# Gated recurrence and tanh-shrink layer: score matmuls of a level issued head by head in turn

## The chip, the cores and the metric

The kernel runs on one core of one Trainium2 chip. The metric is the device time of one execution in microseconds, the median of several runs. A core has five engines that work at the same time, each on its own queue of instructions in order: TensorE (PE in the profile; its weight loads are shown apart as PEld), VectorE (DVE), ScalarE (ACT), GpSimd (POOL) and SyncE (SP, which here only starts DMAs).

## The reference

There are two blocks. The first is a gated linear recurrence over 768 tokens for 4 batches of 8 heads with 48 features each. The second is a dense layer from 384 to 2048 and back, with h - tanh(h) between.

```python
for t in range(S):
    state = alpha[:, :, t, :, None] * state + einsum('bhd,bhe->bhde', k[:, :, t], v[:, :, t])
    y[:, :, t] = einsum('bhd,bhde->bhe', q[:, :, t], state)
x = y.transpose(0, 2, 1, 3).reshape(B * S, H * D)      # (3072, 384)
h = x @ w_in                                           # w_in (384, 2048)
out = (h - tanh(h)) @ w_out                            # w_out (2048, 384)
```

All arithmetic is fp32. The weights come as float64 and are rounded to fp32 on the chip.

## The kernel before

**Tiling.** The 3072 tokens are cut into 12 units of 256 tokens (two chunks of 128). For each unit, `gla(u)` computes the recurrence and leaves x with features on the partitions (`xT`), and `moe(u)` runs the dense layer on it. `load(u)` starts the DMAs of a unit, and `weights()` loads and converts the two weight matrices once, while the first units run.

**The recurrence.** A head's 48 features are padded to 64 rows, so that two heads lie on the 128 partitions: even heads (`hh` = 0) on rows 0 to 63, odd heads (`hh` = 1) on rows 64 to 127. Two chunks by four pairs of heads give G = 8 groups. `flip` transposes alpha, k and q into `pre`, `kT` and `qT`. Within a chunk, the decays between tokens are built by halving, in seven levels. At each level:

- VectorE forms `W` from `qT` times `pre` (L209) and `kT` times `suf` (L213);
- TensorE multiplies, for each of 8 groups and each half of the rows, 64 by 128 weights from `W` with 64 columns of `W` (L220), into a PSUM tile `sc` that holds 8 groups of 64 columns, one whole bank;
- VectorE copies the entries that the mask selects from `sc` into `scores` (L225), once for even and once for odd heads;
- GpSimd brings `suf` and `pre` to the next level (L234, L235).

The pool `ps_sc` has two buffers, so a level's tile for even heads takes the buffer that the level before used for its even heads, and so for odd heads. All eight PSUM banks are in use. After the levels, `scores` and the state from chunk to chunk are multiplied with q and v into `y` (L246, L249), and the state is carried on (L261 to L279).

**The dense part.** `moe(u)` has eight steps. Each makes `h` for 256 of the 2048 hidden features (L292: 12 TensorE instructions), computes h - tanh(h) by a polynomial on ScalarE and VectorE (L301 to L310), and, two steps later, adds to the output tiles `o` (L317: 8 instructions).

**Order.** A list written out at the end of the kernel interleaves the pieces: the recurrence of unit u is handed over beside the dense steps of unit u - 1. The framework's scheduler then fixes each engine's order of instructions at build time and inserts the semaphores; it may move an independent instruction ahead of another. At run time each engine follows that order.

Of the kernel before, what the change touches and what calls it, by code (L numbers as in the profile page):

```python
# [8 lines left out]
FP32 = mybir.dt.float32  # L9
I32 = mybir.dt.int32  # L10
# [4 lines left out]
PSUM = bass.MemoryType.PSUM  # L15

P = 128
HP = 64         # rows that a head's features take up on the partitions
CU = 2          # chunks of 128 tokens in a unit

# h - tanh(h) = h u Q(u) with u = h h. Q to the last bit of fp32 for u <= U_MAX; past that
# the difference itself has lost little.
U_MAX = 0.25
C0, C1, C2, C3, C4 = 0.3333333280927353, -0.1333322737626519, 0.05393378726557631, -0.021472710399165713, 0.006946984308285347
ZA = C4 ** 0.5
# [5 lines left out]
def kernel(  # L31
# [11 lines left out]
    B, H, S, D = q.shape  # L43
    HD = H * D
    NP = H // 2
    G = CU * NP
    TU = CU * P
    UPB = S // TU
# [15 lines left out]
    ps_sc = ctx.enter_context(tc.tile_pool(name="ps_sc", bufs=2, space=PSUM))  # L64
# [5 lines left out]
    V, A, T, GP = nc.vector, nc.scalar, nc.tensor, nc.gpsimd  # L70
# [5 lines left out]
    m_bias = consts.tile([P, 1], FP32, name="m_bias")  # L76
    V.memset(m_bias, -U_MAX)

    # mask[s, l, t]: token s is in the left half of the block of 2 << l whose right half has
    # t, the t-th token of right halves.  # L80
    mask = consts.tile([P, LEVELS, P // 2], FP32, name="mask")
    GP.memset(mask, 1.0)
    for l in range(LEVELS):
        L = 1 << l
        m = mask[:, l, :].rearrange("p (n j) -> p n j", j=L)
        n = P // (2 * L)
# [2 lines left out]
        GP.affine_select(out=m, in_=m, compare_op=ALU.is_ge, fill=0.0, base=L - 1,  # L89
                         pattern=[[2 * L, n], [0, L]], channel_multiplier=-1)  # L90

    # What only parts of are written later: features past D of a head, scores of s >= t, and
    # the state between the heads of a pair stay 0.
    nat = [[consts.tile([P, CU, H, HP], FP32, name=f"{n}{i}") for n in ("an", "kn", "qn")]
           for i in range(2)]
    for i in range(2):
# [2 lines left out]
    scores = [consts.tile([P, 2, G, P], FP32, name=f"scores{i}") for i in range(2)]  # L99
# [7 lines left out]
    w_out = consts.tile([P, FT, d_model], FP32, name="w_out")  # L107

    def load_w(dst, src):
        """A part of a weight matrix, of up to 512 columns: from float64 rounded to fp32, with  # L110
        what fp32 has no normal number for as 0 or infinite."""
        if moe_w_in.dtype == FP32:
            nc.sync.dma_start(out=dst, in_=src)
            return
        n = dst.shape[-1]
        raw = two.tile([P, 512], I64, name="raw")
        nc.sync.dma_start(out=raw[:, 0:n], in_=src)
        words = raw.bitcast(I32).rearrange("p (n w) -> p n w", w=2)
        lo, hi = words[:, 0:n, 0].bitcast(mybir.dt.uint32), words[:, 0:n, 1]
        e = two.tile([P, 512], I32, name="e", tag="u")[:, 0:n]  # L120
        m = two.tile([P, 512], I32, name="m", tag="z")[:, 0:n]
        low = two.tile([P, 512], FP32, name="low", tag="t")[:, 0:n]
        man = two.tile([P, 512], FP32, name="man", tag="w")[:, 0:n]
        V.tensor_scalar(out=e, in0=hi, scalar1=20, scalar2=0x7FF,  # L124
                        op0=ALU.logical_shift_right, op1=ALU.bitwise_and)
        V.tensor_scalar(out=e, in0=e, scalar1=896, scalar2=1151, op0=ALU.max, op1=ALU.min)
        V.tensor_scalar(out=e, in0=e, scalar1=23, scalar2=0x3FFFFFFF,  # L127
                        op0=ALU.logical_shift_left, op1=ALU.bitwise_and)
        V.scalar_tensor_tensor(out=e, in0=hi, scalar=-0x40000000, in1=e,  # L129
                               op0=ALU.bitwise_and, op1=ALU.bitwise_or)  # L130
        V.tensor_single_scalar(out=m, in_=hi, scalar=0xFFFFF, op=ALU.bitwise_and)  # L131
        A.activation(man, m, AF.Copy, bias=1.0, scale=2.0 ** -20)
        A.activation(low, lo, AF.Copy, scale=2.0 ** -52)
        GP.tensor_add(man, man, low)
        V.tensor_mul(dst, man, e.bitcast(FP32))

    def weights():
        """In the order in which the first unit needs them."""
        w = 512
        for i in range(d_ff // w):  # L140
            for j in range(KT):
                load_w(w_in[:, j, i * w:(i + 1) * w], w_in_r[:, j, i * w:(i + 1) * w])
            yield
            for f in range(i * w // P, (i + 1) * w // P):
                load_w(w_out[:, f, :], w_out_r[:, f, :])
            yield
# [3 lines left out]
    def load(u):  # L150
        b, i = divmod(u, UPB)
        vt = three.tile([P, CU, H, D], FP32, name="vt")
        for c in range(CU):
            t0 = i * TU + c * P
# [8 lines left out]
    xT = {}  # L163

    def gla(u):
        """x of a unit's tokens, features on the partitions. Within a chunk of 128 tokens, s and
        t > s part at one level of halving: s in a block's left half, t in its right one. The
        decay between them is then one product from the middle to t times one from s to the
        middle, each of factors that the recurrence itself multiplies."""
        b, i = divmod(u, UPB)  # L170
        an, kn, qn = nat[u % 2]
        vt = loaded.pop(u)
# [2 lines left out]
        def unit(name, pool=two):  # L175
            return pool.tile([P, CU, NP, P], FP32, name=name)

        def halves(t, L):
            x = t.rearrange("p c g (n two j) -> p (c g n) two j", two=2, j=L)
            return x[:, :, 0, :], x[:, :, 1, :]  # L180

        def flip(dst, src, copy):
            tp = ps_tp.tile([P, NP, P], FP32, name="tp")
            for g in range(NP):
                T.transpose(tp[:, g, :], src[:, 2 * g:2 * g + 2, :], ident)  # L185
            copy(dst, tp)

        pre, suf, qT, kT = unit("pre"), unit("suf"), unit("qT"), unit("kT")
        for c in range(CU):
            flip(pre[:, c], an[:, c], V.tensor_copy)  # L190
            flip(kT[:, c], kn[:, c], A.copy)
            flip(qT[:, c], qn[:, c], A.copy)
        # s = t
        qk = two.tile([P, CU * H, D], FP32, name="qk")
        dv = two.tile([P, CU * H, D], FP32, name="dv")
        dot = two.tile([P, CU * H], FP32, name="dot")
# [7 lines left out]
        for l in range(LEVELS):  # L204
            L = 1 << l
            W = unit("W")
            (W0, W1), (k0, _), (_, q1) = halves(W, L), halves(kT, L), halves(qT, L)
            (p0, p1), (s0, s1) = halves(pre, L), halves(suf, L)
            V.tensor_mul(W1, q1, p1)  # L209
            if l == 0:  # L210
                A.copy(W0, k0)
            else:
                V.tensor_mul(W0, k0, s0)  # L213
            Wh = W.rearrange("p c g (n two j) -> p (c g) n two j", two=2, j=L)
            Wf = W.rearrange("p c g t -> p (c g) t")
            for hh in range(2):
                rows = slice(HP * hh, HP * hh + HP)
                sc = ps_sc.tile([P, G, P // 2], FP32, name="sc")
                for g in range(G):
                    T.matmul(sc[:, g, :], lhsT=Wf[rows, g, :], rhs=Wh[rows, g, :, 1, :],  # L220
                             start=True, stop=True)
                to = P_[:, hh].rearrange("p g (n two j) -> p g n two j", two=2, j=L)[:, :, :, 1, :]
                n = P // (2 * L)
                on = mask[:, l, :].rearrange("p (n j) -> p n j", j=L).bitcast(I32)
                V.copy_predicated(  # L225
                    out=to, mask=on.unsqueeze(1).to_broadcast([P, G, n, L]),
                    data=sc.rearrange("p g (n j) -> p g n j", j=L))
            e0 = p0[:, :, L - 1:L].to_broadcast(list(p0.shape))
            e1 = p1[:, :, L - 1:L].to_broadcast(list(p1.shape))
            if l == 0:  # L230
                GP.tensor_copy(s0, p1)
                GP.memset(s1, 1.0)
            else:
                GP.tensor_mul(s0, s0, e1)  # L234
            GP.tensor_mul(p1, p1, e0)  # L235
            yield

        x_t = xT[u] = two.tile([P, KT, TU], FP32, name="xT")
        for c in range(CU):
            n = i * CU + c  # L240
            old, new = states[n % 2], states[(n + 1) % 2]
            y = ps_y.tile([P, HD], FP32, name="y", tag="y")
            if n > 0:
                V.tensor_mul(qT[:, c], qT[:, c], pre[:, c])
                for g in range(NP):
                    T.matmul(y[:, 2 * g * D:2 * (g + 1) * D], lhsT=qT[:, c, g, :],  # L246
                             rhs=old[:, g, :], start=(g == 0), stop=False, skip_group_check=True)
            for h in range(H):
                T.matmul(y[:, h * D:(h + 1) * D], lhsT=P_[:, h % 2, c * NP + h // 2, :],  # L249
                         rhs=vt[:, c, h, :], start=(n == 0 and h == 0), stop=True,  # L250
                         skip_group_check=True)
            x = two.tile([P, HD], FP32, name="x")
# [14 lines left out]
            up = ps_y.tile([P, NP, 2 * D], FP32, name="up", tag="y")  # L267
            for g in range(NP):
                T.matmul(up[:, g, :], lhsT=ks[:, g, :],  # L269
                         rhs=vt[:, c, 2 * g:2 * g + 2, :], start=(g == 0), stop=(g == NP - 1),  # L270
                         skip_group_check=True)
            for hh in range(2):
                at = (slice(HP * hh, HP * hh + HP), slice(None), slice(D * hh, D * hh + D))
                if n == 0:
                    V.tensor_copy(new[at], up[at])
                    continue
                end = pre[at[0], c, :, P - 1:P].to_broadcast([HP, NP, D])
                GP.tensor_mul(new[at], old[at], end)  # L278
# [51 lines left out]
            nc.sync.dma_start(out=out_r[u * CU + c], in_=ob)  # L330
        yield

    # The order in which instructions are handed to the scheduler: a unit's own recurrence runs
    # while the unit before it is in the dense part.
    MOE, GLA, EARLY = FS + 1, 1 + LEVELS + 2 * CU, 5.0
    order = []
    for u in range(NU):
        order += [(u * MOE + i, 1, "moe", u) for i in range(MOE)]
        at = (u - 1) * MOE - EARLY
# [39 lines left out]
```

## Time and profile before

| | |
|---|---|
| Median of 3 runs | 1139.68 us (1138.49 to 1145.95) |
| Profiled execution, span | 1140.3 us; no other time of this execution is given |
| Instructions | 14741 |
| TensorE matmul busy | 1045.0 us (92%) |
| VectorE busy | 805.0 us (71%) |
| GpSimd busy | 342.8 us (30%) |
| ScalarE busy | 320.6 us (28%) |
| Mean granted TensorE clock | 0.909 of full |
| Score matmuls (L220) | 2688 instructions, 305 ns mean each, 338.1 us busy |
| Copies out of the score tiles (L225) | 168 of 882 ns mean, 147.8 us busy |

Busy time is the union of the times in which an engine had an instruction in progress. Matmuls overlap in the pipeline, so the mean time of one is longer than the pitch from one to the next. "Granted clock" is the share of TensorE's full clock that the chip allowed. In lists of waits, the engine and line on the left waited for those on the right: microseconds in total, how often, the longest. A row of the timeline gives the start, the length, the engine, the line, the operation and the count of instructions merged into it.

### The profile page before, as it was taken

What the parts mean: (1) busy time and instruction counts of PE and PEld (TensorE: products, weight loads), DVE (VectorE), ACT (ScalarE), POOL (GpSimd) and SP (SyncE); (2) the same over time, 40 slices, a digit from 0 to 9 for tenths busy, and PEclk for the clock granted to TensorE, in tenths of its full rate; (3) what the DMA queues carried; (4) which work ended last, traced back from release to release, by engine and by line L of the source; (5) the groups of instructions that cost most, each with busy time, mean ns of one, the idle gap of its engine ahead of it and who ended that gap; (6) DMA issues with size and microseconds to landing.
All of it is one profiled execution on the core that took longest, in us unless ns stands there. A gap on an engine that the chain in (4) does not pass through costs nothing.

```text
span 1140.3 us, 14741 instructions
## 1 busy us (share of the span) xinstructions
PE 1045.0 (92%) x5752; PEld 845.6 (74%) x5752; DVE 805.0 (71%) x1212; ACT 320.6 (28%) x569; POOL 342.8 (30%) x293
## 2 busy tenths in 40 slices
PE   3765648999999999999999999999999999999988
PEld 2764548877877878778777788778787788777765
DVE  6688896584684677776774777685775676776766
ACT  2012330321421331421511431521502322413433
POOL 6454443043042044043132043143132152141000
PEclk9999755887998899989988999998979999989999
DMA  9433620110110020110200110200200000000000
GB/s 175 81 91 97 150 73 1 27 30 14 27 31 14 1 56 15 29 28 15 56 1 15 35 23 14 50 8 14 56 1 15 1 1 15 1 1 15 1 14 14
DMA packets 107396, 37.11 MB, mean 33 GB/s; under 512 B 100672, under 2 KB 103744, under 8 KB 107328
## 3 DMA queue, kind: packets, MB, share of 16 engines
q1 hardware_dynamic: 107328, 36.19, 14.1%
q8 instruction: 45, 0.74, 0.3%
q14 instruction: 23, 0.19, 0.1%
HBM read 31.46 MB, written 4.72 MB: 32 GB/s over the span
## 4 chain that ended last, share of the span: by engine, by line
PE 79%; DVE 15%; POOL 2%; issue 2%; ACT 1%; DMA 0%; SPq 0%; POOLq 0%; DVEq 0%
PE sc L220 24%; PE h L292 24%; PE o L317 20%; PE y L249 4%; DVE scores L225 3%; PE tp L185 2%; PE y L246 2%; PE up L269 2%; DVE e L129 1%; DVE W L209 1%; DVE z L307 1%; DVE e L127 1%; PE tp L265 1%; DVE m L131 1%; DVE e L124 1%
## 5 line engine op out<-in xcount | busy, mean ns | idle before, releaser
L220 PEld LDWEIGHTS sc<-W 64*128 64x128 f32 x2688 | 324.9, 217 | 92.7 <-issue 68.7
L220 PE MATMUL sc<-W 64*128 64x64 f32 x2688 | 338.1, 305 | 53.6 <-DVE W L213 41.0
L292 PE MATMUL h<-xT,w_in 128*128 128x256 f32 x1152 | 325.1, 426 | 5.1 <-DVE g L310 3.8
L317 PE MATMUL o<-w_out,g 128*128 128x384 f32 x768 | 278.7, 504 | 0.2 <-DVE g L310 0.2
L292 PEld LDWEIGHTS h<-xT,w_in 128*128 128x128 f32 x1152 | 231.7, 213 | 46.0 <-issue 4.8
L225 DVE COPY_PREDICATED scores<-mask,sc 128x512 f32<-128x512 int32 x168 | 147.8, 882 | 117.4 <-PE sc L220 115.1
L317 PEld LDWEIGHTS o<-w_out,g 128*128 128x128 f32 x768 | 147.5, 198 | 84.0 <-issue 7.7
L301 ACT ACTIVATE sq<-h 128x512 f32<-128x512 f32 x96 | 57.4, 598 | 440.9 <-PE h L292 437.1
L235 POOL TENSOR_TENSOR pre<-pre 128x512 f32<-128x512 f32 x84 | 118.3, 1409 | 115.5 <-DVE W L209 112.3
L234 POOL TENSOR_TENSOR suf<-suf,pre 128x512 f32<-128x512 f32 x72 | 100.3, 1393 | 140.3 <-DVE W L213 137.5
L305 DVE TENSOR_TENSOR w<-h,sq 128x512 f32<-128x512 f32 x96 | 66.2, 690 | 93.1 <-ACT th L302 92.4
L209 DVE TENSOR_TENSOR W<-qT,pre 128x512 f32<-128x512 f32 x84 | 60.1, 716 | 24.9 <-POOL pre L235 14.9
L310 DVE COPY_PREDICATED g<-large,h 128x512 f32<-128x512 int32 x96 | 70.6, 736 | 3.3
L309 DVE SCALAR_TENSOR_TENSOR g<-z,w 128x512 f32<-128x512 f32 x96 | 70.8, 737 | 1.8
L307 DVE SCALAR_TENSOR_TENSOR z<-z,sq 128x512 f32<-128x512 f32 x96 | 70.2, 731 | 0.0
L303 ACT ACTIVATE z<-sq,z_bias 128x512 f32<-128x512 f32 x96 | 69.6, 725 | 0.0
L304 ACT ACTIVATE large<-sq,m_bias 128x512 f32<-128x512 f32 x96 | 69.3, 722 | 0.0
L308 DVE SCALAR_TENSOR_TENSOR z<-z,sq 128x512 f32<-128x512 f32 x96 | 67.7, 705 | 1.9
L306 DVE TENSOR_TENSOR h<-h,th 128x512 f32<-128x512 f32 x96 | 66.7, 695 | 0.0
L213 DVE TENSOR_TENSOR W<-kT,suf 128x512 f32<-128x512 f32 x72 | 56.4, 784 | 14.2 <-POOL suf L234 14.2
L278 POOL TENSOR_TENSOR state<-state,pre 64x192 f32<-64x192 f32 x32 | 23.1, 722 | 139.3 <-DVE state L279 69.8
L249 PE MATMUL y<-vt,scores 128*128 128x48 f32 x384 | 53.2, 291 | 4.7 <-DVE scores L225 4.7
(60 smaller groups left out, 737.1 us busy)
## 6 DMA issues: line engine op xcount, KB each, us to landing
raw<-in_moe_w_in_dram SPq DMA_DIRECT2D x12, 512.0 KB, 3.9
raw<-in_moe_w_out_dram SPq DMA_DIRECT2D x16, 384.0 KB, 3.1
an<-in_alpha_dram SPq DMA_DIRECT2D x24, 192.0 KB, 3.3
kn<-in_k_dram SPq DMA_DIRECT2D x24, 192.0 KB, 3.5
qn<-in_q_dram SPq DMA_DIRECT2D x24, 192.0 KB, 3.1
vt<-in_v_dram SPq DMA_DIRECT2D x24, 192.0 KB, 3.9
out_dram<-ob SPq DMA_DIRECT2D x24, 192.0 KB, 1.9
```

The costliest lines, as they stand in the source:

```text
L209: V.tensor_mul(W1, q1, p1)
L220: T.matmul(sc[:, g, :], lhsT=Wf[rows, g, :], rhs=Wh[rows, g, :, 1, :], start=True, stop=True)
L225: V.copy_predicated(out=to, mask=on.unsqueeze(1).to_broadcast([P, G, n, L]), data=sc.rearrange("p g (n j) -> p g n j", j=L))
L234: GP.tensor_mul(s0, s0, e1)
L235: GP.tensor_mul(p1, p1, e0)
L249: T.matmul(y[:, h * D:(h + 1) * D], lhsT=P_[:, h % 2, c * NP + h // 2, :], rhs=vt[:, c, h, :], start=(n == 0 and h == 0), stop=True, skip_ ...
L292: T.matmul(h[:, a, :], lhsT=w_in[:, j, f * P:(f + 1) * P], rhs=x_t[:, j, :], start=(j == 0), stop=(j == KT - 1))
L303: A.activation(z, sq, AF.Square, bias=z_bias, scale=ZA)
L307: V.scalar_tensor_tensor(out=z, in0=z, scalar=ZK, in1=sq, op0=ALU.add, op1=ALU.mult)
L309: V.scalar_tensor_tensor(out=g, in0=z, scalar=C0, in1=w, op0=ALU.add, op1=ALU.mult)
L310: V.copy_predicated(out=g, mask=large.bitcast(I32), data=h)
L317: T.matmul(o[c], lhsT=g[:, a * TU + c * P:a * TU + (c + 1) * P], rhs=w_out[:, f, :], start=(f == 0), stop=(f == FT - 1))
```

## The change

Before, a level ran the even heads' eight matmuls into one PSUM tile and copied it out, and then did the same for the odd heads with the other tile. Now both tiles are taken at the start of the level; the matmuls go through the groups and, for each group, issue the even head and then the odd one; the two copies follow after all 16. Operands, shapes and results are the same. Comments were dropped from the file in the same edit, with the line numbers kept up to this place.

```diff
-            for hh in range(2):
-                rows = slice(HP * hh, HP * hh + HP)
-                sc = ps_sc.tile([P, G, P // 2], FP32, name="sc")
-                for g in range(G):
-                    T.matmul(sc[:, g, :], lhsT=Wf[rows, g, :], rhs=Wh[rows, g, :, 1, :],
-                             start=True, stop=True)
+            sc = [ps_sc.tile([P, G, P // 2], FP32, name="sc") for hh in range(2)]
+            for g in range(G):
+                for hh in range(2):
+                    rows = slice(HP * hh, HP * hh + HP)
+                    T.matmul(sc[hh][:, g, :], lhsT=Wf[rows, g, :], rhs=Wh[rows, g, :, 1, :],
+                             start=True, stop=True)
+            n = P // (2 * L)
+            on = mask[:, l, :].rearrange("p (n j) -> p n j", j=L).bitcast(I32)
+            for hh in range(2):
                 to = P_[:, hh].rearrange("p g (n two j) -> p g n two j", two=2, j=L)[:, :, :, 1, :]
-                n = P // (2 * L)
-                on = mask[:, l, :].rearrange("p (n j) -> p n j", j=L).bitcast(I32)
                 V.copy_predicated(
                     out=to, mask=on.unsqueeze(1).to_broadcast([P, G, n, L]),
-                    data=sc.rearrange("p g (n j) -> p g n j", j=L))
+                    data=sc[hh].rearrange("p g (n j) -> p g n j", j=L))
```

## The prediction

> **What bounds the kernel now.** I read the page's busy times and chain first, then the span by stages, then single bursts in the timeline.
>
> ```profile
> span 1140.3 us, 14741 instructions
> ...
> PE 1045.0 (92%) x5752; PEld 845.6 (74%) x5752; DVE 805.0 (71%) x1212; ACT 320.6 (28%) x569; POOL 342.8 (30%) x293
> ...
> PE 79%; DVE 15%; POOL 2%; issue 2%; ACT 1%; DMA 0%; SPq 0%; POOLq 0%; DVEq 0%
> PE sc L220 24%; PE h L292 24%; PE o L317 20%; PE y L249 4%; DVE scores L225 3%; PE tp L185 2%; PE y L246 2%; PE up L269 2%; DVE e L129 1%; DVE W L209 1%; DVE z L307 1%; DVE e L127 1%; PE tp L265 1%; DVE m L131 1%; DVE e L124 1%
> ```
>
> TensorE is the bound, and the score matmuls (sc, L220), the only lines that change, are a quarter of the chain. I cut the span by what TensorE does. From 233.5 to 1042 us ten stretches with the seven score bursts of a unit alternate with stretches without any. The columns are stretch, length, then busy time (count) of PE, PEld, DVE, ACT, POOL, then the granted clock.
>
> ```profile
> 233.50:288.00 54.50, 54.24 (x298) 42.28 (x298) 35.22 (x49) 9.29 (x17) 22.28 (x16) 0.81 0.04 11
> ...
> 410.00:456.00 46.00, 46.00 (x300) 37.18 (x300) 36.89 (x50) 9.21 (x17) 22.10 (x16) 0.96 0.04 13
> ...
> sum 499.50, PE 494.88 PEld 398.49 DVE 345.33 ACT 92.54 POOL 211.14; mean PE 49.49 PEld 39.85 DVE 34.53 ACT 9.25 POOL 21.11
> ```
>
> That sum is over the ten burst stretches: 499.5 us, TensorE busy in 494.9, VectorE in 345.3. So in them a microsecond less of TensorE work is a microsecond less of time, until VectorE, at 34.5 us in each, is what ends last. Two stretches of like work differ by their clock: 54.5 x 0.81 and 46.0 x 0.96 both come to 44.2 us, which I take as TensorE's need in one stretch at full clock. Outside these, the units' other stretches and the last 98 us hold no bursts, and before 208 us TensorE mostly waits.
>
> **What one burst costs, and why.** The timeline (start, length, engine, line, count) shows a level's 16 fp32 matmuls as 32 instructions, two for each matmul, each with a weight load of its own:
>
> ```profile
> 410.17 3.42 PE L220 MATMUL sc<-W 64*128 64x64 f32 x32
> 413.52 2.93 PE L317 MATMUL o<-w_out,g 128*128 128x384 f32 x4
> 416.24 1.31 PE L292 MATMUL h<-xT,w_in 128*128 128x256 f32 x4
> 417.49 3.39 PE L220 MATMUL sc<-W 64*128 64x64 f32 x32
> 420.81 1.99 PE L292 MATMUL h<-xT,w_in 128*128 128x256 f32 x8
> ```
>
> Each uses 64 of the array's rows: even heads the lower 64, odd heads the upper. Before the change all 16 even instructions are issued, then all 16 odd ones. The next view counts score instructions in three stretches of equal length within the burst that starts at 319.99, the middle one at the change from even to odd:
>
> ```profile
> 320.50:320.90 0.40, 0.40 (x6) 0.40 (x6) 0.00 (x0) 1.00 0.01 0
> 321.38:321.78 0.40, 0.40 (x10) 0.40 (x9) 0.00 (x0) 1.00 0.00 0
> 322.30:322.70 0.40, 0.40 (x6) 0.40 (x5) 0.21 (x1) 1.00 0.00 0
> ```
>
> Ten instructions are in flight or start in the middle one against six elsewhere. So even and odd instructions already run at the same time at the seam, and the four extra ones say how many: the last four even with the first four odd. The pitch follows from the burst and one instruction's own time (the middle of least/median/most ns, over all):
>
> ```profile
> L220 PE MATMUL sc<-W x2688: 268/272/473, 25.5 to 1042.0; 64*128 64x64 f32 x192
> ```
>
> 3.39 less the last one's 0.27 is 3.12 us for 32 - 4 = 28 steps, 0.111 us each. Two of a pitch of 0.111 at a time is 0.056 us each.
>
> **The change part by part.** Nothing is removed or added: 16 matmuls, 2 copies (L225) and 2 tiles per level stay. Moved are the matmuls (even, odd, even, odd within a level), the first copy (behind all 16 matmuls instead of behind eight), and the second tile's taking (to the level's start). No DMA and no POOL operation changes its place; the SP queue is not touched.
>
> The burst: both row halves always have work, so 28 steps become 16, and 12 x 0.111 = 1.34 us are saved per burst at full clock. Bounds for this: 0 if the array pairs them only as the four at the seam are paired now, 12 x 0.111 at full pairing. I take the latter, since the middle row above is the nearest: it is the same instruction pair on the same rows of the array. TensorE's need in a burst stretch falls from 44.2 to 44.2 - 7 x 1.34 = 34.8 us.
>
> The clock: bursts also cost clock now.
>
> ```profile
> 410.00:413.40 3.40, 3.40 (x33) 3.23 (x32) 2.88 (x4) 1.34 (x3) 3.30 (x3) 1.00 0.24 49
> 413.40:416.80 3.40, 3.40 (x8) 1.98 (x8) 3.30 (x6) 0.00 (x0) 1.94 (x2) 0.50 0.00 0
> ```
>
> A 3.4 us stretch filled by one burst (33 instructions, TensorE busy throughout) is followed by one at half clock, in which only eight dense instructions fit. A burst of 2.0 us leaves room for dense work in the same stretch, so I expect few such drops. This gain is inside the 44.2 already. The Trainium skill (TensorE: Matmul & The Clock Gate, Part 1) puts the drop to half clock down to an idle window; here TensorE was busy for all 3.40 us before it, so the trace does not agree. By the page's rule bursts would not cost clock, and TensorE's need would stay stretched by the mean clock.
>
> What is late next is VectorE. Its waits from 208 to 1042 us:
>
> ```profile
> DVE scores L225 <- PE sc L220: 94.4, 59, 5.7
> ...
> DVE W L209 <- POOL pre L235: 14.5, 16, 1.2
> DVE W L213 <- POOL suf L234: 13.1, 13, 1.3
> DVE kT L261 <- POOL suf L234: 11.2, 10, 1.5
> ...
> DVE qT L244 <- POOL pre L235: 7.6, 8, 1.0
> ```
>
> The 94.4 us for bursts is slack that TensorE's speed removes. The four waits for POOL, 46.4 us or 4.6 per stretch, belong to the decay products of the recurrence (VectorE multiply, POOL update, VectorE multiply) and do not shrink. So VectorE needs 34.5 + 4.6 = 39.1 us per stretch, above TensorE's 34.8. I add 0.9 for waits for bursts that stay (a tenth of 9.4): **40 us** per burst stretch, and 499.5 - 400 = 99.5 us saved.
>
> The added wait: a level's second matmul now needs the tile that the previous level's second copy reads. Behind it in TensorE's queue stand the rest of the burst and the dense work.
>
> ```profile
> 412.20 2.74 DVE L225 COPY_PREDICATED scores<-mask,sc 128x512 f32<-128x512 int32 x2 [0.52 <-PE sc L220]
> ...
> 449.51 2.86 PE L292 MATMUL h<-xT,w_in 128*128 128x256 f32 x12
> ```
>
> Two copies take up to 2.74 us back to back (while POOL works), and 2.86 is the dense work between two bursts at its shortest in this stretch. So the wait is just covered; it costs nothing if VectorE starts the copies at once and up to 0.7 us (one copy at its shortest, 1.4 for two) in a level where other VectorE work is queued ahead of them. The 0.9 above stands for this too.
>
> Before 208 us (first two recurrences, clock at half) VectorE is the busier engine and waits for bursts:
>
> ```profile
> 39.63 6.26 PE L220 MATMUL sc<-W 64*128 64x64 f32 x32 [2.59 <-DVE W L213]
> ...
> 43.31 0.71 DVE L225 COPY_PREDICATED scores<-mask,sc 128x512 f32<-128x512 int32 x1 [0.21 <-PE sc L220]
> 45.93 0.69 DVE L225 COPY_PREDICATED scores<-mask,sc 128x512 f32<-128x512 int32 x1 [1.91 <-PE sc L220]
> ```
>
> ```profile
> DVE scores L225 <- PE sc L220: 10.6, 10, 1.9
> ```
>
> ```profile
> DVE scores L225 <- PE sc L220: 10.2, 8, 1.8
> ```
>
> The last two rows are the waits in 25 to 116 and 116 to 208 us: 20.8 us in 14 bursts. Less one instruction's 0.42 (the mean in the row below), a burst of 6.26 has 28 steps of 0.209, and falls by 12 x 0.209 = 2.5 to 3.8 us.
>
> ```profile
> L220 PE MATMUL sc<-W 64*128 64x64 f32 x224 | 42.9, 419 | 21.1 <-DVE W L213 17.0 <-DVE W L209 4.2
> ```
>
> The second copy's wait (1.91) goes; the first's grows, since it can start at 3.8 instead of about 3.4 us. Of 1.5 us per burst I take 0.6 as saved, 14 x 0.6 = 8 us (bounds 0 and 20.8).
>
> The stretches without bursts:
>
> ```profile
> sum 334.50, PE 331.11 PEld 261.80 DVE 231.03 ACT 144.71 POOL 36.93; mean PE 33.11 PEld 26.18 DVE 23.10 ACT 14.47 POOL 3.69
> ```
>
> They are TensorE-bound without score work; I give them 2 us for clock drops that a burst just before them causes. **Sum:** 1140.3 - 99.5 - 8 - 2 = 1031 us. The profiled execution's span is 0.6 us above the median shown (1139.68), so no correction is due.
>
> **The rivals.** *TensorE stays the bound* (chance 0.2): VectorE fills all waits for POOL with dense-part work, and a burst stretch takes 34.8 + 1.2 = 36 us. Against it stand the waits for POOL within the 46 us stretch, where such work was at hand too:
>
> ```profile
> DVE W L209 <- POOL pre L235: 1.6, 2, 1.0
> DVE W L213 <- POOL suf L234: 1.0, 1, 1.0
> DVE kT L261 <- POOL suf L234: 0.9, 1, 0.9
> ```
>
> Time: 1140.3 - 139.5 - 12 = 989 us.
>
> *VectorE holds up TensorE more* (0.18): the order of instructions is fixed at build time for another balance, a late copy or W stalls TensorE, its clock drops in the gap, and a stretch takes 45 us. For it speak the longest stretches beside the first, which are those with the lowest clock and up to 2 us of idle TensorE:
>
> ```profile
> 320.00:373.00 53.00, 51.99 (x300) 42.10 (x299) 33.72 (x49) 9.63 (x18) 20.30 (x14) 0.87 0.03 9
> ...
> 569.50:626.00 56.50, 54.49 (x300) 43.61 (x299) 34.15 (x49) 9.64 (x18) 19.75 (x14) 0.82 0.03 9
> ...
> 824.80:878.00 53.20, 53.12 (x298) 43.04 (x298) 33.85 (x48) 9.61 (x18) 19.73 (x14) 0.84 0.03 9
> ```
>
> Time: 1140.3 - 49.5 - 4 = 1087 us. The Trainium skill (TensorEngine Tiling (Array Packing), PSUM Bottleneck) says of tiling that it speeds up TensorE but not the emptying of PSUM, whose copy may become the limit; VectorE's 0.7 to 1.3 us a copy here are of that kind.
>
> *The change does not do what it says* (0.08): pairing beyond the four at the seam fails, because TensorE's queue is not filled at 0.056 us per load and matmul; nothing in the trace shows that rate over a whole burst, only eight instructions of it. Bursts stay at 3.1 to 3.6 us; with what the later first copy costs, 1140 us.
>
> *Slower* (0.08): pairing fails, and both tiles of a level are wanted at once, so that TensorE waits for the previous level's second copy. It decides wherever the dense work between two bursts is shorter than two copies (2.86 against 2.74 above, no margin). At half a microsecond in 70 levels and 0.4 in the 14 early ones that is 35 + 6: 1181 us.
>
> **How the numbers follow.** The forecast (VectorE-bound burst stretches of 38 to 43 us: 1011 to 1061) has 0.46. The range goes from 980 (below the TensorE-bound case, since its 36 us may be 35) to 1100 (the third case with 46 us a stretch); outside lie the last two cases and a little of the others. About 1% is what a measurement here can tell from no change. Faster by over 1%: 0.46 + 0.2 + 0.18 = 0.84; within 1%: 0.08; slower: 0.08.
>
> **What would show it.** Right: bursts of x32 in 1.9 to 2.1 us at full clock and in 3.7 to 3.9 at half; twelve or so instructions per 0.40 us throughout; burst stretches near 40 us with VectorE busy near 90% in them; a granted clock above 0.95 there; the waits of L225 for sc down to a third of 94.4. Wrong: bursts still over 3 us, or TensorE waiting often for "DVE scores L225" ahead of L220. What would make the number wrong with the mechanism right is the new order of the dense work between bursts, which the profile of before cannot show.

## The result, and the profile after

The changed kernel takes 1046.3 us (median of 4 runs, 1044.9 to 1055.7) against 1139.1 us before; the ratio is 0.921, with a 95% interval of 0.915 to 0.927. Forecast were 1031 us, with a range of 980 to 1100. The profiled execution has a span of 1045.6 us. Each experiment below ran the kernel before again beside it, and its ratio is to those runs; ratios leave out executions more than 1.5% above the fastest of the same kernel, which the medians keep.

The page's busy times, and the chain by engine and by line:

```profile
span 1045.6 us, 14688 instructions
...
PE 925.5 (89%) x5752; PEld 725.9 (69%) x5752; DVE 806.5 (77%) x1212; ACT 322.3 (31%) x569; POOL 332.4 (32%) x293
...
PE 68%; DVE 23%; issue 3%; POOL 2%; ACT 2%; DMA 0%; SPq 0%; POOLq 0%; DVEq 0%
PE h L293 23%; PE o L318 20%; PE sc L220 13%; DVE scores L226 5%; PE y L250 4%; DVE W L209 3%; PE tp L185 2%; DVE z L308 2%; PE y L247 2%; PE up L270 2%; DVE W L213 1%; DVE w L306 1%; DVE h L307 1%; DVE z L309 1%; DVE e L129 1%
```

The score matmuls' share of the chain fell from 24% to 13%, TensorE's busy time by 119.5 us; VectorE's own work did not change and stands for more of the chain. (L225 is L226 now, L234 and L235 are L235 and L236.) The timeline has both kinds of bursts that are left:

```profile
25.48 3.68 PE L220 MATMUL sc<-W 64*128 64x64 f32 x32 [2.70 <-DVE W L209]
...
389.05 2.00 PE L220 MATMUL sc<-W 64*128 64x64 f32 x32
390.98 1.99 PE L293 MATMUL h<-xT,w_in 128*128 128x256 f32 x8
393.25 3.39 PE L220 MATMUL sc<-W 64*128 64x64 f32 x32 [0.28 <-DVE scores L226]
```

The burst at 389.05 takes 2.00 us where a burst at full clock took 3.4 before, and the one at 25.48 takes 3.68 us at half clock, where 6.26 was usual before. The one at 393.25 is as long as before. Score instructions in stretches of 0.40 us within the first of the two, in the same columns as in the prediction:

```profile
389.30:389.70 0.40, 0.40 (x12) 0.40 (x10) 0.00 (x0) 1.00 0.00 0
389.70:390.10 0.40, 0.40 (x12) 0.40 (x10) 0.00 (x0) 1.00 0.00 0
390.10:390.50 0.40, 0.40 (x12) 0.40 (x12) 0.00 (x0) 1.00 0.00 0
```

Twelve throughout, against six before: two streams at the old pitch, over the whole burst. Now the time by stages. First the stretches with bursts, cut anew at the new bursts (two of the ten rows, and the sum of all ten), then the sum of the ten without, then the long view from 210 us to the last burst, before and after:

```profile
219.00:268.00 49.00, 47.53 (x317) 35.92 (x315) 35.98 (x53) 10.17 (x18) 21.02 (x16) 0.86 0.04 12
...
600.00:644.00 44.00, 41.98 (x315) 32.50 (x315) 38.64 (x53) 9.19 (x17) 20.78 (x16) 0.92 0.04 13
...
sum 465.50, PE 444.48 PEld 339.17 DVE 376.20 ACT 96.42 POOL 198.72; mean PE 44.45 PEld 33.92 DVE 37.62 ACT 9.64 POOL 19.87
```

```profile
sum 292.00, PE 292.00 PEld 231.82 DVE 210.17 ACT 141.48 POOL 35.80; mean PE 29.20 PEld 23.18 DVE 21.02 ACT 14.15 POOL 3.58
```

```profile
210.00:1042.00 832.00, 824.00 (x4742) 658.83 (x4740) 576.37 (x852) 235.63 (x420) 248.07 (x194) 0.93 0.09 21
```

```profile
210.00:951.00 741.00, 719.98 (x4680) 557.69 (x4679) 573.24 (x840) 232.34 (x411) 231.68 (x191) 0.94 0.11 23
```

The two sums together went from 834 to 757.5 us, 76.5 less, which is most of the 95 us of the whole; the scheduler moved some dense work into the stretches with bursts, so the two kinds can only be compared together. The granted clock rose only from 0.93 to 0.94; in the stretches with bursts alone it was 0.90, after 0.89 before (the mean of the ten rows, weighted by length). In time, the trace's list of clock changes has 92 us at half clock from 210 us on, after 123 before. TensorE stood idle for 8 us before and for 21 us after. This is what it waited for, and VectorE's wait for bursts:

```profile
PE sc L220 <- DVE scores L226: 10.6, 14, 1.4
PE sc L220 <- DVE W L209: 10.4, 6, 1.7
```

```profile
DVE scores L226 <- PE sc L220: 25.4, 26, 1.9
```

The first line is the added wait, on the previous level's copies. Both views are from 210 us on; before that, TensorE waited another 23.0 us for the previous level's copies (6 times, 6.5 us the longest), where it had not waited for them in the kernel before.

### The profile page after: what moved, and what is told of

Same layout as the page of the kernel before. It is cut to its first block, busy times and chain, and to the rows that moved or that the text cites. A ratio compares the mean times of both kernels' runs of the same rounds, so it can differ in the third digit from the quotient of the medians.

```text
span 1045.6 us, 14688 instructions
## 1 busy us (share of the span) xinstructions
PE 925.5 (89%) x5752; PEld 725.9 (69%) x5752; DVE 806.5 (77%) x1212; ACT 322.3 (31%) x569; POOL 332.4 (32%) x293
## 4 chain that ended last, share of the span: by engine, by line
PE 68%; DVE 23%; issue 3%; POOL 2%; ACT 2%; DMA 0%; SPq 0%; POOLq 0%; DVEq 0%
PE h L293 23%; PE o L318 20%; PE sc L220 13%; DVE scores L226 5%; PE y L250 4%; DVE W L209 3%; PE tp L185 2%; DVE z L308 2%; PE y L247 2%; PE up L270 2%; DVE W L213 1%; DVE w L306 1%; DVE h L307 1%; DVE z L309 1%; DVE e L129 1%
## 5 line engine op out<-in xcount | busy, mean ns | idle before, releaser
L293 PE MATMUL h<-xT,w_in 128*128 128x256 f32 x1152 | 316.3, 414 | 3.8 <-DVE g L311 3.8
L220 PE MATMUL sc<-W 64*128 64x64 f32 x2688 | 230.8, 302 | 80.4 <-DVE scores L226 33.6
L220 PEld LDWEIGHTS sc<-W 64*128 64x128 f32 x2688 | 216.2, 214 | 121.9 <-issue 61.3
L293 PEld LDWEIGHTS h<-xT,w_in 128*128 128x128 f32 x1152 | 221.4, 205 | 38.9 <-issue 4.2
L226 DVE COPY_PREDICATED scores<-mask,sc 128x512 f32<-128x512 int32 x168 | 141.9, 880 | 38.0 <-PE sc L220 37.9
L235 POOL TENSOR_TENSOR suf<-suf,pre 128x512 f32<-128x512 f32 x72 | 93.5, 1299 | 182.9 <-DVE W L213 181.8
L236 POOL TENSOR_TENSOR pre<-pre 128x512 f32<-128x512 f32 x84 | 111.9, 1332 | 55.0 <-DVE W L209 50.7
L209 DVE TENSOR_TENSOR W<-qT,pre 128x512 f32<-128x512 f32 x84 | 66.0, 785 | 17.0 <-ACT qT L186 8.9
L308 DVE SCALAR_TENSOR_TENSOR z<-z,sq 128x512 f32<-128x512 f32 x96 | 78.9, 822 | 0.0
L309 DVE SCALAR_TENSOR_TENSOR z<-z,sq 128x512 f32<-128x512 f32 x96 | 70.7, 736 | 2.1
L303 ACT ACTIVATE th<-h 128x512 f32<-128x512 f32 x96 | 57.1, 594 | 0.0
```

Source lines behind the costliest of these rows:

```text
L220: T.matmul(sc[hh][:, g, :], lhsT=Wf[rows, g, :], rhs=Wh[rows, g, :, 1, :], start=True, stop=True)
L226: V.copy_predicated(out=to, mask=on.unsqueeze(1).to_broadcast([P, G, n, L]), data=sc[hh].rearrange("p g (n j) -> p g n j", j=L))
L293: T.matmul(h[:, a, :], lhsT=w_in[:, j, f * P:(f + 1) * P], rhs=x_t[:, j, :], start=(j == 0), stop=(j == KT - 1))
L308: V.scalar_tensor_tensor(out=z, in0=z, scalar=ZK, in1=sq, op0=ALU.add, op1=ALU.mult)
L309: V.scalar_tensor_tensor(out=z, in0=z, scalar=C1, in1=sq, op0=ALU.add, op1=ALU.mult)
```

## The experiments

Theory A was the prediction's: the two row halves of the array work at the same time, and that is the gain. Its rival B: the new order that the scheduler found, with early tiles and late copies, is the gain. For what was left to explain, theory C said that VectorE's work now bounds the stretches with bursts, and D that waits, unpaired bursts and clock drops do.

**Without pairing, in the same order.** Only the rows that the odd heads' matmuls read are changed; every engine's order of instructions stays that of the changed kernel.

```diff
-                    rows = slice(HP * hh, HP * hh + HP)
+                    rows = slice(0, HP)
```

> Edit: the odd heads' matmuls read rows 0 to 63 too, so their scores are those of the even heads. Every engine keeps the order of instructions of the changed kernel; only two row halves at a time are gone. Theory A (the gain is pairing of the row halves in the array): a burst of 32 takes 32 x 0.111 + 0.27 + 0.05 = 3.8 us instead of 2.0, and the kernel loses about 1.7 us in each of some 68 paired bursts: 1140 to 1180 us. Theory B (the gain comes from the new order that the scheduler found and the earlier tiles): bursts do not matter, 1040 to 1055 us.

Measured: 1190.8 us, ratio to before 1.044 (1.037 to 1.050). One of its bursts in the timeline:

```profile
430.19 3.78 PE L220 MATMUL sc<-W 64*128 64x64 f32 x32
```

The same order with one row half at a time gives 3.78 us a burst, as expected (32 steps, without even the four pairs that the kernel before had), and loses the whole gain. B falls. The time is 11 us above A's range, and the clock from 210 us on says where to look:

```profile
210.00:1088.00 878.00, 876.67 (x4726) 704.08 (x4724) 584.46 (x852) 235.43 (x417) 234.21 (x194) 0.89 0.09 20
```

The trace has 189 us at half clock in it, against 92 in the changed kernel: longer bursts cost more than their own length.

**Without the turns.** Early tiles and late copies as in the change, the matmuls in the old order.

```diff
-            for g in range(G):
-                for hh in range(2):
+            for hh in range(2):
+                for g in range(G):
```

> Edit: both tiles taken at once and both copies behind all 16 matmuls, as in the changed kernel, but all even heads first, then all odd ones. Theory A: bursts of 3.4 us as before the change, and the later first copy costs a little or nothing: 1135 to 1175 us. Theory B (early tiles and late copies carry the gain): 1040 to 1060 us.

Measured: 1142.4 us, 1.0005 (0.997 to 1.005). This is as A says, but it is no test of B. In the trace, every engine has the kernel before's order of operations, from the first to the last: with the matmuls in the old order, the scheduler put tiles and copies back where they had been. What early tiles and late copies cost by themselves was not measured. That B falls rests on the run above and on "One tile without the turns" below, which keep a new order and take the pairing away.

**One tile of two banks.** The burst at 393.25 above is long because the scheduler handed out even heads first while the odd heads' tile was still taken. In the timeline 16 of the 84 bursts are of this kind, 6 of the first 14 and then one in every unit. One tile for both halves takes this freedom away.

```diff
-    ps_sc = ctx.enter_context(tc.tile_pool(name="ps_sc", bufs=2, space=PSUM))
+    ps_sc = ctx.enter_context(tc.tile_pool(name="ps_sc", bufs=1, space=PSUM))
...
-            sc = [ps_sc.tile([P, G, P // 2], FP32, name="sc") for hh in range(2)]
+            sc2 = ps_sc.tile([P, 2, G, P // 2], FP32, name="sc")
+            sc = [sc2[:, hh] for hh in range(2)]
```

> Edit: one PSUM tile of two banks for a level, so that the scheduler cannot issue even heads ahead while the odd heads' tile is taken; in the changed kernel it did so in 16 of 84 bursts. Theory A: every burst takes 2.0 us (3.7 at half clock); 10 x 1.4 us saved in the steady part, some us before it: 1025 to 1040 us. Rival: the head start of the even heads was worth as much, TensorE now waits longer for the second copy: 1047 to 1065 us.

Measured: **1006.7 us**, 0.883 (0.878 to 0.889), the fastest version here that leaves no work out, and faster than either expectation. All 84 bursts are of the short kind, except the few that a clock drop lengthens. Two of its ten stretches with bursts and the sum of all, the long view, and TensorE's waits there:

```profile
219.50:262.00 42.50, 38.43 (x305) 29.22 (x305) 38.30 (x52) 8.50 (x16) 20.97 (x16) 0.92 0.04 13
...
652.00:693.50 41.50, 37.46 (x316) 28.79 (x315) 37.29 (x53) 9.63 (x18) 20.80 (x16) 1.00 0.06 15
...
sum 417.50, PE 389.18 PEld 297.97 DVE 368.57 ACT 95.04 POOL 197.17; mean PE 38.92 PEld 29.80 DVE 36.86 ACT 9.50 POOL 19.72
```

```profile
210.00:909.00 699.00, 670.66 (x4669) 521.36 (x4668) 568.75 (x838) 231.64 (x411) 229.76 (x191) 0.97 0.11 25
```

```profile
PE sc L221 <- DVE scores L227: 14.9, 11, 2.3
PE sc L221 <- DVE W L209: 10.5, 6, 1.8
PE sc L221 <- DVE W L213: 2.7, 1, 2.7
```

The waits did grow, as the rival said, from 21 to 28 us, but the time at half clock went from 92 to 41 us, and ten bursts lost 1.4 us each. 14 us for the bursts and half of 51 for the clock, less 7 for the waits, are 33 of the 40 us; the rest is not told apart.

**Four at a time.** In the version with one tile the order inside a burst can be changed and every engine's order outside it stays the same.

```diff
-            for g in range(G):
-                for hh in range(2):
+            for g0, hh, gi in [(g0, hh, gi) for g0 in range(0, G, 4) for hh in range(2) for gi in range(4)]:
+                if True:
+                    g = g0 + gi
```

> Edit: as the run with one tile of two banks, but four even matmuls (eight instructions), four odd, four even, four odd. Theory A with a short look-ahead (four instructions pair at each change of halves, as in the trace of before): three changes, 12 pairs, 20 steps: bursts of 20 x 0.111 + 0.05 + 0.27 = 2.5 us, and 0.5 us x 70 = some 35 us above the run with one tile. If the look-ahead is deep, bursts of 2.0 us and the same time as the run with one tile.

Measured: 1039.5 us, 0.911 (0.905 to 0.918), 33 us above the run with one tile.

```profile
251.72 2.60 PE L222 MATMUL sc<-W 64*128 64x64 f32 x32
```

That is 2.60 us, near the 2.5 of the short look-ahead: only about four instructions of a stream pair with the next one at each change of halves. Turns of one matmul (two instructions) keep both streams fed; turns of four do not.

**One tile without the turns.** The same, with all eight even heads first (`gg` is 0 for the even heads and 8 for the odd ones).

```diff
-            for g in range(G):
-                for hh in range(2):
-                    rows = slice(HP * hh, HP * hh + HP)
+            for gg in range(0, 2 * G, 8):
+                for g in range(gg // (2 * 8) * 8, gg // (2 * 8) * 8 + 8):
+                    hh = gg // 8 % 2; rows = slice(HP * hh, HP * hh + HP)
```

> Edit to the version with one tile of two banks: all eight even heads, then all eight odd ones. Every engine's order outside the bursts is that of the alternating version, so the difference from its 1007 us is pairing alone. Theory A (pairing carries the gain): bursts of 3.4 us instead of 2.0; the run with four at a time lost 33 us for 0.6 us a burst, so 1.39 us cost 33 x 1.39 / 0.6 = 76 us or, with more clock drops, up to 115: 1083 to 1122 us. Rival (most of the 1007 is a better order around the bursts): 1010 to 1050 us.

Measured: 1141.8 us, 0.999 (0.994 to 1.003). So in the order that gives 1007 us with pairing, the kernel without pairing is where it was before the change: all of the gain, some 131 us by the ratios (0.999 less 0.883), is pairing, with the clock that hangs on it. I had expected 1083 to 1122. The cost grows faster than the burst's length: 0.6 us more a burst cost 33 us, 1.39 us more cost 131. The clock is the reason that the traces show: from the third recurrence's first burst to the end of the last, the run with four at a time was at half clock for 44 us, about as long as the version with one tile (41), and this one for 154 (in a profiled execution of 1153.8 us).

**Less VectorE work.** One operation of the polynomial is left out of three versions.

```diff
-            V.scalar_tensor_tensor(out=z, in0=z, scalar=C1, in1=sq, op0=ALU.add, op1=ALU.mult)
```

> Edit to the kernel before the change: one of the polynomial's VectorE operations (the one with C1, 96 of 705 ns, 68 us in all) is left out, so h - tanh(h) is not computed in full. If TensorE bounds the kernel before, as the prediction said: at most 1% less, 1127 to 1140 us. If VectorE bounds it: 1138 - 60 = some 1078 us.

Measured: 1166.7 us, 1.023 (1.016 to 1.029): slower with less work. VectorE was not the bound, but the order is new. From 210 us on:

```profile
210.00:1073.00 863.00, 858.69 (x4742) 686.44 (x4740) 529.98 (x773) 236.22 (x419) 247.09 (x194) 0.88 0.09 20
```

In it are 208 us at half clock, against 123 before. Half of the 85 us more is 43, which covers the 28 us lost; that the new order put bursts so as to lower the clock is read from this and was not tested apart.

> The same operation left out of the changed kernel (96 of 736 ns, 71 us). Theory C (as predicted, VectorE bounds the stretches with bursts): about half of the 71 us lies there, so 30 us less, 1010 to 1020 us. Theory D (waits at the second copy, bursts that the scheduler did not pair and the clock drops that follow bound it): less than 12 us less, 1035 to 1047 us.

Measured: 1021.7 us, 0.896 (0.889 to 0.903): 25 us less than the changed kernel, between both expectations. The trace says where most of it is from: between the third recurrence's first burst and the end of the last, it took 701.8 us in place of 728.5, with 55 us at half clock in place of 92. That is worth 19 of the 27 us.

> The same operation left out of the version with one tile of two banks (all bursts paired, 1007 us, VectorE busy 88% in the stretches with bursts). Theory C: VectorE is the bound there, 25 to 35 us less: 972 to 982 us. Theory D: TensorE's own work is the bound there too, less than 12 us less: 995 to 1007 us.

Measured: 994.2 us, 0.873 (0.867 to 0.878): 12.5 us less than with one tile, for 70 us less VectorE work. This is at the edge of D and far from C. Between the third recurrence's first burst and the end of the last, only 4 us are gained (686.9 to 682.8 us), and 7 us less at half clock and 3 us less idle time of TensorE cover them, although VectorE was busy for 52 us less from 210 us on. Each of these runs has an order of its own, and the first of them shows that an order can be worth 28 us, so they do not settle how much VectorE's load costs; they speak against VectorE as the bound of the stretches with bursts.

**ScalarE empties the tile.**

```diff
+            sb = consts.tile([P, 2, G, P // 2], FP32, name="sb")
+            A.copy(sb, sc2)
...
-                    data=sc[hh].rearrange("p g (n j) -> p g n j", j=L))
+                    data=sb[:, hh].rearrange("p g (n j) -> p g n j", j=L))
...
-            x = two.tile([P, HD], FP32, name="x")
+            x = consts.tile([P, HD], FP32, name="x")
```

> Edit to the version with one tile of two banks: ScalarE copies the tile to SBUF at once, and VectorE's two masked copies read that copy (x has one buffer instead of two, to make room). TensorE then waits for a ScalarE copy of about 1 us and not for VectorE's queue. If the wait for the copies (40 us of TensorE's idle time there, 15 of it after 219 us) is on the path: 980 to 1000 us. If VectorE's own work is the bound, the wait only moves: 1000 to 1012 us; ScalarE's queue, which also makes the squares and tanh of the dense part, may add to it.

Measured: 1077.4 us, 0.946 (0.938 to 0.953), 71 us slower than with one tile. Two groups and two of TensorE's waits of this run:

```profile
L229 DVE COPY_PREDICATED scores<-mask,sb 128x512 f32<-128x512 int32 x168 | 181.2, 1129 | 14.9 <-ACT sb L224 14.9
L224 ACT COPY sb<-sc 128x1024 f32<-128x1024 f32 x84 | 85.0, 1012 | 241.5 <-DVE scores L229 177.4 <-PE sc L221 61.4 <-DVE z L311 2.7
```

```profile
PE sc L221 <- DVE W L213: 53.9, 14, 13.4
PE o L321 <- DVE g L314: 35.0, 11, 5.3
```

The masked copy takes 1129 ns in the mean from SBUF where it took 882 from PSUM. The middle one is nearly as fast (748 ns against 716); more of the copies are slow ones, 81 of 168 over 1 us against 48, and the runs do not show why. ScalarE waited 177 us for the single SBUF buffer to come free. The wait moved, and VectorE became later for everything else: between the third recurrence's first burst and the end of the last, TensorE was idle for 70 us in place of 28 and at half clock for 96 in place of 41, which is 42 + 27 = 69 of the 71 us. Whether two buffers would do better was not run.

**One copy, and the lead of the recurrence.** Three more orders of the version with one tile: a single masked copy over both banks, and the recurrence handed over 4 or 6 dense steps ahead instead of 5 (of these two, the diff of the run with 4 is shown).

```diff
-            for hh in range(2):
-                to = P_[:, hh].rearrange("p g (n two j) -> p g n two j", two=2, j=L)[:, :, :, 1, :]
-                V.copy_predicated(
-                    out=to, mask=on.unsqueeze(1).to_broadcast([P, G, n, L]),
-                    data=sc[hh].rearrange("p g (n j) -> p g n j", j=L))
+            to = P_.rearrange("p h g (n two j) -> p (h g) n two j", two=2, j=L)[:, :, :, 1, :]
+            V.copy_predicated(
+                out=to, mask=on.unsqueeze(1).to_broadcast([P, 2 * G, n, L]),
+                data=sc2.rearrange("p h g (n j) -> p (h g) n j", j=L))
```

> Edit to the version with one tile of two banks: one masked copy over both banks (128x1024) instead of two of 128x512. If VectorE's fixed cost per instruction counts: 84 x 0.06 us = 5 us less, 1000 to 1004 us. The scheduler makes a new order; such orders have moved the time by up to 2% with nothing else to explain it, so 985 to 1030 us.

```diff
-    MOE, GLA, EARLY = FS + 1, 1 + LEVELS + 2 * CU, 5.0
+    MOE, GLA, EARLY = FS + 1, 1 + LEVELS + 2 * CU, 4.0
```

> Edit to the version with one tile of two banks: the recurrence is handed over 4 dense steps ahead instead of 5. If only the pairing and the clock matter, the same within 1.5%: 992 to 1022 us. A better fit of the bursts to the dense work would show as fewer clock drops than 47 us after the first 210.

> Edit to the version with one tile of two banks: the recurrence is handed over 6 dense steps ahead instead of 5. The same within 1.5%, 992 to 1022 us, with more or fewer clock drops as the order falls.

Measured: 1025.4 us (0.902, 0.897 to 0.906), 1019.7 us (0.898, 0.892 to 0.904) and 1039.1 us (0.914, 0.908 to 0.920). The single copy does save VectorE time:

```profile
L226 DVE COPY_PREDICATED scores<-mask,sc 128x1024 f32<-128x1024 int32 x84 | 134.8, 1605 | 12.2 <-PE sc L221 12.2
```

134.8 us against 141.0 in the version with two copies. Yet all three are slower than that version, by 1.3 to 3.2%: the 1000 to 1004 us that the saved VectorE time alone would give did not come, and the last run is beyond what I expected. Between the third recurrence's first burst and the end of the last, TensorE was idle for 37 to 43 us in them, against 28, and at half clock for 48 to 68 us, against 41. The order around the bursts is worth as much as 30 us, and 1007 us is the best of the four orders tried, not a law of that version.

## Why the prediction was right, and which of its steps were not

- **The burst.** 12 steps of 0.111 us, 1.34 us off, was right: a burst went from 3.39 to 2.00 us (1.39 off), and takes 3.68 at half clock against 3.8 forecast. The seam of before had shown it. The queue, whose filling was open, keeps up with 0.056 us per load and matmul over a whole burst: the rival in which pairing fails is out, and with it the one that ends slower.
- **Seven short bursts in a stretch.** This was wrong by one: the term 7 x 1.34 was 6 x 1.39. The prediction said that the order would be new and did not see that two tiles let the scheduler unpair a level. The run with one tile shows what that cost, together with its clock: up to 40 us, more than the 15 us by which the forecast missed.
- **The clock.** This is the step that failed. Above 0.95 was expected in the stretches with bursts; it was 0.90 there, nearly unchanged from 0.89. From 219 us on, the trace lists 20 drops to half clock, two in every unit, of 3.4 or 6.8 us each. One of either kind shows in two pairs of 3.4 us stretches of the changed kernel:

```profile
379.80:383.20 3.40, 1.66 (x26) 1.39 (x26) 3.40 (x5) 0.00 (x0) 1.47 (x2) 1.00 0.00 0
383.20:386.60 3.40, 3.40 (x17) 2.73 (x16) 3.40 (x4) 0.28 (x1) 2.02 (x3) 0.51 0.00 0
393.50:396.90 3.40, 3.40 (x34) 3.31 (x34) 2.46 (x5) 0.00 (x0) 0.00 (x0) 1.00 0.02 5
396.90:400.30 3.40, 3.40 (x8) 2.22 (x7) 2.47 (x5) 1.91 (x4) 1.50 (x2) 0.50 0.01 2
```

The first drop follows a stretch in which TensorE was busy for 1.66 of 3.40 us (it waited 1.74 us for W), the second one filled by the unpaired burst. All 20 are of these two kinds. Ten follow 3.4 us in which TensorE was busy for 1.7 to 2.0 us (48 us at half clock), and ten follow 3.4 us in which it was busy for 3.0 to 3.4 us, mostly with the unpaired burst (44 us). With one tile, eight drops are left from 219 us on (41 us), all behind stretches with TensorE busy for 0.9 to 2.2 us, and the clock in the stretches with bursts was 0.95. So the prediction was right that a short burst with dense work beside it costs no clock. What it put at nothing were the gaps, in which TensorE waits for W and for the copies, and the level that is not paired.

- **VectorE as the next bound.** The forecast had 40 us per stretch from 34.5 of work, 4.6 of waits for POOL and 0.9. Burst and other stretch together were forecast as 40 + 33.25 = 73.3 us and measured as 75.8; with one tile, 72.0 from the first burst of one unit to that of the next (219.8 to 867.6 us in nine units). The length came near, the reason did not hold. VectorE was busy 81% of the stretches, not 90, and 88% with one tile, and there a tenth less of its work gave 12.5 us in place of 25 to 35. The waits for POOL, which were said not to shrink, fell from 46.4 to 31.6 us. TensorE's own work, its 21 to 28 us of waits and the clock account for more of the length. The Trainium skill's warning (TensorEngine Tiling (Array Packing), PSUM Bottleneck) that the emptying of PSUM may become the limit agrees with the traces only in so far as TensorE came to wait for the copies, 10.6 us from 210 us on.
- **The added wait.** A tenth of 9.4 us per stretch was allowed, and 10.6 us in ten stretches were measured: right. The 23.0 us before 210 us were not foreseen. VectorE's wait for bursts fell to 25.4 us, a little under the third of 94.4 that was expected.
- **Before 208 us.** 8 us were forecast; the third recurrence's first burst starts at 219.5 us instead of 233.7, 14 us earlier, although 6 of the first 14 bursts are unpaired. VectorE's waits for bursts fell there from 20.8 to 12.4 us, which is the forecast's term; the other 6 us are not told apart. The half clock of this part is read from the instructions' own time (419 ns against 272); the granted clock of the profile's rows is 1.00 from 25 to 116 us.

The sum was near because two errors were of opposite sign. Between the third recurrence's first burst and the end of the last, 99.5 + 2 us were forecast as saved, and 80.0 were (808.5 to 728.5 us). Sixty short bursts of 1.39 us and half of the 31 us less at half clock, less 13 us more of idle time, come to 86, so the terms named above more than cover it. The start gained 6 us more than forecast. The rival in which VectorE holds up TensorE and the clock drops in the gap acted here: its 45 us would make 78.3 us of both stretches together (45 + 33.25), and the measured 75.8 lies halfway between that and the forecast's 73.3. That the whole came much nearer to the forecast than to this rival is owed mostly to the start, and is luck. (The 12 and the 4 us beside the stretches in the times of the first two rivals have no working; the forecast has 8 + 2 there.)

## What to carry to other kernels

When matmuls use half of the array's rows, issue the two halves in turn, one matmul each: here the stream ran at twice its rate (0.056 in place of 0.111 us per load and matmul). This is shown for fp32 matmuls of 64 by 128 weights with 64 columns, whose halves write different PSUM banks; one bank for both was not run. Look for a seam between two row halves in the trace first; it shows the gain before anything is built. Then make sure that the scheduler cannot undo the turns, by giving it one buffer for both halves (40 us here), and try a few orders around it, since an order alone moved this kernel by up to 3%.

## What the runs showed of the hardware that I had not expected

- Instructions of the other row half start before the first half's are done: in the kernel before, the first odd one started 6 ns after the fourth-last even one. With turns of four matmuls a burst took 2.60 us, with turns of one 2.00.
- The granted clock fell to half after 3.4 us stretches that TensorE filled with score matmuls of one row half at a time (34 instructions, busy all the time, then 0.50), and not only after partly idle ones; with all bursts paired, no drop from 219 us on followed a stretch in which TensorE was busy for more than 2.2 us. Bursts of one half at a time cost twice: 1.39 us more in each of 70 bursts is 97 us, and with the clock they cost some 131.
- Less VectorE work, in a new order, made the kernel 2.3% slower, with the clock from 210 us on at 0.88 in place of 0.93.
- A masked copy of 128x512 took 1129 ns in the mean when it read SBUF and 882 when it read PSUM, in two versions that differ in more than this.
